# Constants on GpSimd, an early loop entry on VectorE, and V's last half in smaller pieces, in a one-query attention over 8192 keys

## The chip, the cores and the metric

The kernel runs on one core of a Trainium2 chip. The metric is the device time of one execution in microseconds (us). The profile is of one execution, and its span is 1.8 us shorter than the time of that execution.

Five engines do the work: TensorE (PE; its weight loads are PEld), VectorE (DVE), ScalarE (ACT), GpSimd (POOL), and SyncE (SP), which here only issues DMAs. Sixteen DMA engines move the data (the page counts in shares of 16, and a piece has 16 landing records).

## The reference

```python
B, H, Sq, Sk, D = 1, 16, 1, 8192, 256          # all bfloat16

def reference(q, k, v):
    scale = q.shape[-1] ** -0.5
    scores = jnp.einsum("bhqd,bhkd->bhqk", q, k) * scale
    p = _softmax(scores, axis=-1)
    return jnp.einsum("bhqk,bhkd->bhqd", p, v)
```

There is one query per head, so every byte of K and V is used once: 16 heads x 2 tensors x 8192 x 256 x 2 bytes = 134.2 MB must be read. There is nearly no arithmetic per byte.

## The kernel before

Each head's K and V are read in two halves of 2 MB. A half lies in SBUF as 128 partitions x 32 columns x 256 elements. The 64 halves go through one issue queue (SyncE): four K halves first, then K and V in turn. There are four K buffers and four V buffers. Some halves are cut into pieces (the numbers are columns):

```python
FIRST_CUT = (4, 4, 8, 16)     # the first half of K
LAST_CUT = (16, 8, 4, 4)      # the last half of V
BEFORE_CUT = (16, 16)         # two V halves before it
...
for i, wd in enumerate(cs):   # one DMA per piece, all from SyncE
    plan.op("sp", lambda e, ...: e.dma_start(
        b[:, at * D : (at + wd) * D], cols(t, h, c + at, c + at + wd)), ..., waits, dma=(s, used[id(s)]))
```

VectorE takes 24 of 32 columns of each K half (product with the broadcast query and a sum, one instruction a column), TensorE the other eight (transposes and matmuls). Then come the softmax over the head's 8192 scores and 64 matmuls with V. VectorE's part is a loop of eight passes over two heads. Ahead of it, VectorE makes the constants that the other engines need (ones, and two identity matrices for TensorE):

```python
dve(lambda e: e.memset(ones_rowb[:, :], 1.0), "c_onesb")
...                                              # an index row by doubling, a transpose, a compare
dve(lambda e: e.tensor_scalar(identb[:, :], colf[:, :], pidx[:, 0:1], None, ALU.is_equal), "c_idb", ["c_p"])
dve(lambda e: e.tensor_scalar(ident[:, :], colf[:, :], pidx[:, 0:1], None, ALU.is_equal), "c_id")
...
with nc.Fori(0, n, 1, engines=[eng.engine], head_slot={eng.engine: 0}):
    for j in range(step):
        ...                                      # the loop's waits and instructions
```

`head_slot` sets the place of the loop's first instruction in the engine's stream of instructions; the code ahead of the loop branches there (VectorE's at 4.43 us in the trace below).

The matmuls with a V half wait piece by piece; `landed` names the pieces that a column needs:

```python
for c in range(c0, c1):
    pe(lambda e, c=c, col=col: e.matmul(a[0:1, 0:D], lhsT=E[:, col : col + 1],
           rhs=Vb[slot][:, c * D : (c + 1) * D], ...),
       ..., [f"e{h}", first_free] + landed("v", n, c, c + 1))
```

## Time and profile before

| what | value | where |
|---|---|---|
| time | 324.89 us, median of 3 | the runs |
| VectorE busy | 277.7 us, 86% | page, part 1 |
| TensorE busy | 220.3 us, 68% | page, part 1 |
| DMA queue of K and V | 98.2% of 16 engines' span | page, part 3 |
| VectorE's first product | 10.75 us | timeline |

From the page of the kernel before: the share of busy DMA engines and the bytes per second in 40 slices of the span, then the K and V queue (packets, MB, share of 16 engines), then the chain of work that ended last.

```profile
DMA  7999999999999999999999999999999999999993
GB/s 276 431 432 424 419 435 430 424 422 430 426 429 430 424 424 430 430 430 428 424 430 428 432 428 422 430 428 429 430 424 426 428 429 435 424 422 432 417 419 128
...
q1 hardware_dynamic: 10368, 134.22, 98.2%
...
DVE 49%; DMA 42%; issue 5%; PE 3%; DVEq 0%; ACT 0%; SPq 0%
```

Two lines here contradict each other. By the queue, the DMA engines are full from the second slice to the last but one. By the chain, half of the span is VectorE's. Both are right as records. The chain goes back from a DMA to what released its issue (VectorE freeing a K buffer), although that DMA then waited in a full queue, which the chain doesn't see (K half 4, issued at 19.36 us, before K half 3 landed, at 22.34 to 24.53). The packet records of this kernel give 428.5 GB/s between 285 and 300 us, if each packet's bytes are spread over its time (the profile's table of stretches, which counts a packet whole where it starts, says 433).

VectorE's start, from the timeline (start, duration, engine, line, operation, and in brackets the idle time before it and what ended it):

```profile
0.81 0.17 DVE L279 MEMSET ones_rowb<- 1x128 bf16 x1 [0.81 <-PEq L728]
...
3.82 0.06 DVE L298 MEMSET lsum<- 128x1 f32 x1
10.75 0.42 DVE L360 CUSTOM_DVE_ANT_0 prod<-Kb,qbc 128x256 bf16<-128x256 bf16 x1 [6.88 <-issue]
```

"issue" means that it waited for nothing that the profile shows. In the records of its sequencer there is a taken branch at 4.43 us and nothing until 10.6.

The DMA issues of the beginning, from the timeline of SyncE. The first row merges eight issues; its last is K half 4, the first that needs a freed buffer, at 19.36 us:

```profile
0.73 18.95 SPq L319 DMA_DIRECT2D Kb<-in_k_dram  x8
19.73 0.43 SPq L319 DMA_DIRECT2D Vb<-in_v_dram  x1
```

The tail, from the timeline of TensorE:

```profile
312.50 3.95 PE L607 MATMUL acc<-Vb,E 128*1 128x256 bf16 x32
317.05 3.65 PE L607 MATMUL acc<-Vb,E 128*1 128x256 bf16 x32 [0.59 <-DMA Vb<-in_v_dram]
```

The last piece landed at 319.50 us, and TensorE ended at 320.70, 1.20 us later. It was held until 317.05 by a piece of 16 columns and then had 32 matmuls to do, 0.109 us each.

### The profile page before, as it was taken

The numbers are of one execution on the slowest core, as the hardware profiler recorded it, in microseconds if no ns is written. First come the engines' busy times: TensorE is split into PE (matmuls) and PEld (weight loads), VectorE is DVE, ScalarE is ACT, GpSimd is POOL, SyncE is SP. The second block draws the span as 40 slices with busy tenths as digits, with TensorE's granted clock in tenths as the row PEclk, the third lists the DMA queues.
The fourth block names the chain that finished last, engine by engine and source line by source line (L and its number), as shares of the span: only waits on it lengthen the run. The fifth ranks groups of instructions, "written<-read, shape, count | busy, mean of one in ns | idle before, by whom it ended". The sixth has DMA issues, their size and how long they took to land.

```text
span 322.8 us, 6456 instructions
## 1 busy us (share of the span) xinstructions
PE 220.3 (68%) x2166; PEld 155.1 (48%) x2166; DVE 277.7 (86%) x1607; ACT 94.1 (29%) x185; POOL 0.2 (0%) x4
## 2 busy tenths in 40 slices
PE   1463428777587848784887658686667866857896
PEld 0332325545456635563565535464444644535574
DVE  3699999999999999999998988889988889888600
ACT  3362321423324242332142242212422213232010
POOL 0000000000000000000000000000000000000000
PEclk9999999979789967999597987977898796998799
DMA  7999999999999999999999999999999999999993
GB/s 276 431 432 424 419 435 430 424 422 430 426 429 430 424 424 430 430 430 428 424 430 428 432 428 422 430 428 429 430 424 426 428 429 435 424 422 432 417 419 128
DMA packets 10415, 134.37 MB, mean 416 GB/s; under 512 B 1170, under 2 KB 1187, under 8 KB 1956
## 3 DMA queue, kind: packets, MB, share of 16 engines
q1 hardware_dynamic: 10368, 134.22, 98.2%
q8 instruction: 5, 0.08, 0.1%
q14 instruction: 6, 0.05, 0.0%
q10 hardware_dynamic: 36, 0.02, 0.0%
HBM read 134.23 MB, written 0.01 MB: 416 GB/s over the span
## 4 chain that ended last, share of the span: by engine, by line
DVE 49%; DMA 42%; issue 5%; PE 3%; DVEq 0%; ACT 0%; SPq 0%
DVE prod L360 46%; DMA Kb<-in_k_dram 27%; DMA Vb<-in_v_dram 15%; PE acc L607 3%; DVE S L360 2%; DVE g L332 0%; DVE colf L286 0%; DVE recip L341 0%; DVE m L379 0%; DVEq L145 0%; ACT o L621 0%; DVEq L138 0%; SPq L319 0%; DVEq L139 0%; DVEq L142 0%
## 5 line engine op out<-in xcount | busy, mean ns | idle before, releaser
L360 DVE CUSTOM_DVE_ANT_0 prod<-Kb,qbc 128x256 bf16<-128x256 bf16 x768 | 269.1, 411 | 24.5 <-DMA Kb<-in_k_dram 15.1
L607 PE MATMUL acc<-Vb,E 128*1 128x256 bf16 x1024 | 144.7, 310 | 8.7 <-DMA Vb<-in_v_dram 8.5
L607 PEld LDWEIGHTS acc<-Vb,E 128*1 128x1 bf16 x1024 | 95.0, 95 | 50.7 <-DMA Vb<-in_v_dram 9.9
L502 ACT ACTIVATE KT<-tp 128x1024 bf16<-128x1024 bf16 x64 | 62.0, 1021 | 118.3 <-PE tp L493 118.3
L360 DVE DVE_READ_ACCUMULATOR2_ANT S<- 128x1 f32 x768 | 56.5, 74 | 0.0
L493 PE MATMUL tp<-identb,Kb 128*128 128x128 bf16 x512 | 38.9, 237 | 7.1 <-DMA Kb<-in_k_dram 7.1
L493 PEld LDWEIGHTS tp<-identb,Kb 128*128 128x128 bf16 x512 | 33.0, 106 | 15.2 <-issue 12.8
L519 PE MATMUL spe<-qcur,KT 128*128 128x1 bf16 x512 | 20.7, 165 | 19.6 <-ACT KT L502 19.6
L558 PE MATMUL misc<-g,ones_row 1*128 1x1 f32 x32 | 7.3, 294 | 35.0 <-DVE g L332 35.0
L519 PEld LDWEIGHTS spe<-qcur,KT 128*128 128x128 bf16 x512 | 16.5, 99 | 24.5 <-ACT KT L502 24.3
L621 ACT ACTIVATE o<-acc,recip 1x256 bf16<-1x256 f32 x16 | 7.4, 465 | 68.7 <-PE acc L607 68.7
L558 PEld LDWEIGHTS misc<-g,ones_row 1*128 1x128 f32 x32 | 5.9, 229 | 38.1 <-DVE g L332 37.8
L547 PE MATMUL misc<-ident,m 128*1 128x128 f32 x34 | 7.1, 293 | 20.4 <-DVE m L379 20.4
L547 PEld LDWEIGHTS misc<-ident,m 128*1 128x1 f32 x34 | 1.9, 82 | 24.0 <-DVE m L379 23.5
L565 ACT ACTIVATE negb<-misc 128x1 f32<-128x1 f32 x16 | 2.7, 171 | 26.0 <-PE misc L558 26.0
L332 DVE TENSOR_REDUCE g<-misc 1x1 f32<-1x128 f32 x17 | 4.7, 274 | 5.2 <-PE misc L547 5.2
L587 PE MATMUL misc<-ones_col,lsum 128*1 128x1 f32 x34 | 3.2, 164 | 5.5 <-ACT E L572 3.6
L572 ACT ACTIVATE E<-S,negb 128x64 bf16<-128x64 f32 x16 | 5.6, 347 | 0.7 <-ACT negb L565 0.2
L341 DVE RECIPROCAL recip<-misc 1x1 f32<-1x1 f32 x17 | 2.6, 151 | 3.7 <-PE misc L587 3.7
L439 ACT ACTIVATE qbc<-qb 128x256 bf16<-128x256 bf16 x14 | 5.6, 399 | 0.0
L532 ACT ACTIVATE S<-spe 128x16 f32<-128x16 f32 x16 | 3.0, 184 | 7.2 <-PE spe L519 7.2
L422 ACT ACTIVATE qb<-tp 128x512 bf16<-128x512 f32 x7 | 3.9, 595 | 3.8 <-PE tp L413 3.8
(29 smaller groups left out, 23.0 us busy)
## 6 DMA issues: line engine op xcount, KB each, us to landing
Kb<-in_k_dram SPq DMA_DIRECT2D x31, 2048.0 KB, 23.7
Vb<-in_v_dram SPq DMA_DIRECT2D x29, 2048.0 KB, 29.2
Vb<-in_v_dram SPq DMA_DIRECT2D x5, 1024.0 KB, 19.0
Kb<-in_k_dram SPq DMA_DIRECT2D x1, 1024.0 KB, 7.1
Kb<-in_k_dram SPq DMA_DIRECT2D x2, 256.0 KB, 2.9
Kb<-in_k_dram SPq DMA_DIRECT2D x1, 512.0 KB, 4.7
Vb<-in_v_dram SPq DMA_DIRECT2D x1, 512.0 KB, 12.8
Vb<-in_v_dram SPq DMA_DIRECT2D x2, 256.0 KB, 13.1
```

The source lines that it names most:

```text
L332: lambda e: e.tensor_reduce(g[0:1, s : s + 1], misc[s][0:1, MT0 : MT0 + P], AX.X, ALU.max),
L360: lambda e, slot=slot, c=c, col=col, h=h, r=(ttr - 1) % PROD: e.tensor_tensor_reduce(out=prod[:, r * D : (r + 1) * D], in0=Kb[slot][:, c * ...
L422: lambda e: e.activation(out=qbc[:, a * D : b * D] if first else qb[:, (a - 2) * D : (b - 2) * D], in_=bank[:, 0 : (b - a) * D], func=ACT. ...
L439: lambda e: e.activation(out=qbc[:, s * D : (s + 1) * D], in_=qb[:, (h - 2) * D : (h - 1) * D], func=ACT.Copy),
L493: lambda e, c=c, hf=hf, i=(b * NH + hf) * P, view=view: e.transpose(view[:, i : i + P], Kb[slot][:, c * D + hf * P : c * D + (hf + 1) * P] ...
L502: lambda e, gn=gn, view=view: e.activation(out=KT[gn % KT_SLOTS][:, :], in_=view[:, 0 : GROUP * D], func=ACT.Copy),
L519: lambda e, b=b, hf=hf, oc=oc, gn=gn: e.matmul(spe[sl(h)][:, oc : oc + 1], lhsT=KT[gn % KT_SLOTS][:, (b * NH + hf) * P : (b * NH + hf + 1) ...
L547: lambda e: e.matmul(misc[s][0:1, MT0 : MT0 + P], lhsT=m[:, s : s + 1], rhs=ident[:, :], start=True, stop=True),
L558: lambda e: e.matmul(misc[s][:, BC0 : BC0 + 1], lhsT=ones_row[0:1, :], rhs=g[0:1, s : s + 1], start=True, stop=True),
L572: lambda e: e.activation(out=E[:, s * J : (s + 1) * J], in_=S[:, s * J : (s + 1) * J], func=ACT.Exp, bias=negb[:, h : h + 1], scale=SCALE, ...
L607: lambda e, c=c, col=col: e.matmul(a[0:1, 0:D], lhsT=E[:, col : col + 1], rhs=Vb[slot][:, c * D : (c + 1) * D], start=(x == 0 and c == 0), ...
L621: lambda e: e.activation(out=o[0:1, h * D : (h + 1) * D], in_=acc[s][0:1, 0:D], func=ACT.Copy, scale=recip[0:1, s : s + 1],),
```

## The change

The change wants VectorE free of preparatory work and of the gap before its loop, and the last data in pieces that let TensorE keep up. GpSimd, idle so far, makes the constants, with one `iota` (column minus partition) and two compares with zero. VectorE's loop head goes to slot 128. V's last half is cut so that no piece is over eight columns. The rest is bookkeeping: GpSimd gets an instruction stream, and VectorE's counter starts at 32 so that the loop's register waits stay positive.

```diff
-LAST_CUT = (16, 8, 4, 4)
+LAST_CUT = (8, 8, 8, 4, 4)
+HEAD_SLOT = {"pe": 0, "dve": 128}
 ...
+        if e in self.ahead:
+            eng.sem_inc(self.sems[e], self.ahead[e])
 ...
-            with nc.Fori(0, n, 1, engines=[eng.engine], head_slot={eng.engine: 0}):
+            with nc.Fori(0, n, 1, engines=[eng.engine], head_slot={eng.engine: HEAD_SLOT[e]}):
 ...
-        dve(lambda e: e.memset(ones_rowb[:, :], 1.0), "c_onesb")
-        ...                                   (all constants of VectorE)
-        dve(lambda e: e.memset(lsum[:, 1:2], 1.0), "e-1")
+        pool(lambda e: e.memset(ones_rowb[:, :], 1.0), "c_onesb")
+        pool(lambda e: e.iota(off[:, :], pattern=[[1, P]], base=0, channel_multiplier=-1, ...), "c_off")
+        pool(lambda e: e.tensor_scalar(identb[:, :], off[:, :], 0.0, None, ALU.is_equal), "c_idb", ["c_off"])
+        pool(lambda e: e.tensor_scalar(ident[:, :], off[:, :], 0.0, None, ALU.is_equal))
+        ...                                   (four memsets)
 ...
+        plan.ahead["dve"] = 32
+            @block.gpsimd
+            def _(e):
+                plan.emit("pool", e)
```

## The prediction

> **What bounds the kernel now.** The DMA engines. The page's queue table gives q1 98.2% of 16 engines' span; the slices show 419 to 435 GB/s from the second slice to the last but one. In the packet records a 16 KB packet takes 611 ns, and from 5 to 312 us 15 or more are practically always in flight: the engines never idle. Each 2 MB piece lands 4.89 us after the last. So the time is: first packet (about 2 us after the start), 134.2 MB at that pace, and a tail. The chain of waits says otherwise (DVE 49%), because it walks through freed K buffers; but K half 4, issued at 19.36 us, still found K half 3 in flight (landing 22.3 to 24.5).
>
> **VectorE enters at once.** The timeline shows VectorE's constants from 0.81 to 3.82 us, register moves until 4.4, a taken branch at 4.43, and nothing until 10.6:[...] (an 8,192-byte instruction packet at 8.79 us, under load).[...] VectorE should start when q's broadcast is ready, at about 3.9 us instead of 10.75: 6.9 us earlier. None of this is on the DMA engines' path: K half 4 is issued near 12.5 instead of 19.4 us, into a queue that is full anyway. Worth: 0.
>
> **A side effect that may count.** The 16 engines do not end together: a piece's 16 landings spread over 1.5 us at K half 1, 2.2 at K half 2, 3.0 at V half 0, and 3.2 at the end. Its steps coincide with instruction packets at 8.79, 13.90 and 33.23 us[...]. The slowest engine gains about 0.9 us of lag at each of the three. One fetch fewer should leave that engine near 2.2 us of lag, so that the next, at 2.6, ends last: estimate 0.5 us off the last landing.
>
> **The last half in pieces.** In the timeline the last 16-column piece lands at 317.00, and TensorE then runs 32 matmuls back to back (0.109 us apart) to 320.70, although the later pieces landed at 318.21, 318.86 and 319.50. With 8 columns first, landing about 315.8, TensorE keeps up and has about 4 matmuls left after the last landing: 0.45 us saved. Eight more packets per engine: estimate 0.07 us.
>
> **GpSimd's constants.** Its memsets take 0.1 us[...]. TensorE needs the identity by about 9.2 us (K transposes start 9.28, when the data lands). Slack enough.
>
> **Sum.** 0.5 + 0.45 - 0.07 = 0.9 us, of 324.89: 324.0 us, range 323.2 to 324.9. Faster by over 2%: 0.01; within 2%: 0.98; slower: 0.01.
>
> **To look for.** VectorE's first product near 3.9 us; 4.89 us per piece unchanged; no instruction packet near 8.8; spread of the last landings about 2.6 us instead of 3.2; TensorE's end about 0.7 us after the last landing instead of 1.2.
>
> **What would make it wrong.** No fetch saved (then 324.4), or it moved to an engine that is late already; a slow iota that stalls both TensorE and VectorE beyond 20 us, when the DMA queue would run dry.

0.5 + 0.45 - 0.07 = 0.88, given as 0.9 us. The 0.07 us for eight packets agrees with the trace before: two packets of 2,048 bytes took 9 ns longer than one of 4,096 (84 and 159 ns, medians), and eight times that is 72 ns. "Fetch" means an 8,192-byte packet that the trace calls an instruction packet. No record names which of the five engines it serves; that these are VectorE's is the author's reading of their times (8.79 us, within VectorE's gap of 4.43 to 10.6).

## The result, and the profile after

The changed kernel took 324.27 us (median of 6 runs, 323.32 to 325.07), the kernel before 325.12 us (median of 6, 324.76 to 326.18). The ratio is 0.9969, with a 95% interval of 0.9948 to 0.999. A ratio in this document is the mean time of one kernel's fast runs over that of the other's in the same rounds, so it is not quite the ratio of the medians that are quoted beside it. The difference itself, about 0.85 us, is small but clear of noise.

The profiled execution happened to be the slowest of the six (325.07 us), so its span of 323.3 us is longer than that of the profile before (322.8). A single trace against a single trace would say that the change does harm.

From the page of the changed kernel, the same lines:

```profile
DMA  7999999999999999999999999999999999999993
GB/s 230 431 438 423 424 430 432 426 424 424 431 432 428 424 432 428 432 426 426 434 430 428 424 428 432 430 430 421 428 432 430 430 423 434 426 428 430 416 417 142
...
q1 hardware_dynamic: 10512, 134.22, 98.2%
...
DMA 56%; DVE 38%; PE 2%; issue 2%; SPq 1%; DVEq 0%; ACT 0%
```

The stream is what it was. Only the first slice differs: 230 GB/s instead of 276. In the chain VectorE's share fell by 11 points and the DMA's rose by 14, but the time has not moved with it.

VectorE's start, the constants on GpSimd, and SyncE's first issues, from the timelines:

```profile
4.09 0.42 DVE L359 CUSTOM_DVE_ANT_0 prod<-Kb,qbc 128x256 bf16<-128x256 bf16 x1 [4.09 <-ACT qbc L421]
```

```profile
0.95 0.23 POOL L286 IOTA off<- 128x128 f32 x1
1.27 0.54 POOL L291 TENSOR_SCALAR identb<-off 128x128 bf16<-128x128 f32 x1
1.77 0.53 POOL L292 TENSOR_SCALAR ident<-off 128x128 f32<-128x128 f32 x1
```

```profile
0.72 13.50 SPq L318 DMA_DIRECT2D Kb<-in_k_dram  x8
14.26 0.43 SPq L318 DMA_DIRECT2D Vb<-in_v_dram  x1
```

VectorE starts 6.7 us earlier, and K half 4 is issued at 13.89 us instead of 19.36. What became of the 6.7 us is in VectorE's waits (total us, times, longest). Before, then after:

```profile
DVE prod L360 <- DMA Kb<-in_k_dram: 15.1, 13, 1.2
DVE prod L360 <- issue: 9.4, 5, 6.9
```

```profile
DVE prod L359 <- DMA Kb<-in_k_dram: 22.9, 20, 1.6
DVE prod L359 <- issue: 1.9, 3, 0.7
```

Its waits without a visible cause, the loop's entry above all, fell by 7.5 us; its waits for K grew by 7.8 us. VectorE, early for data that come at a fixed pace (here 4.89 us a half), only waits somewhere else. In these two traces its last product even ends later after the change (304.31 us) than before (303.31).

The tail of the changed kernel, from TensorE's weight loads, which show its two short waits:

```profile
315.53 3.36 PEld L604 LDWEIGHTS acc<-Vb,E 128*1 128x1 bf16 x32 [0.41 <-DMA Vb<-in_v_dram]
319.29 1.61 PEld L604 LDWEIGHTS acc<-Vb,E 128*1 128x1 bf16 x16 [0.40 <-DMA Vb<-in_v_dram]
```

Here the last piece landed at 320.53 us and TensorE ended at 321.20, 0.67 us later instead of 1.20.

### The profile page after: what moved, and what is told of

Same layout as the page of the kernel before. It is cut to its first block, busy times and chain, and to the rows that moved or that the text cites. A ratio compares the mean times of both kernels' runs of the same rounds, so it can differ in the third digit from the quotient of the medians.

```text
span 323.3 us, 6446 instructions
## 1 busy us (share of the span) xinstructions
PE 223.0 (69%) x2166; PEld 155.7 (48%) x2166; DVE 275.6 (85%) x1586; ACT 94.1 (29%) x185; POOL 1.9 (1%) x12
## 3 DMA queue, kind: packets, MB, share of 16 engines
q1 hardware_dynamic: 10512, 134.22, 98.2%
## 4 chain that ended last, share of the span: by engine, by line
DMA 56%; DVE 38%; PE 2%; issue 2%; SPq 1%; DVEq 0%; ACT 0%
DMA Kb<-in_k_dram 41%; DVE prod L359 36%; DMA Vb<-in_v_dram 15%; PE acc L604 2%; DVE S L359 1%; SPq L318 1%; DVE g L331 0%; DVE recip L340 0%; ACT o L618 0%; DVE m L378 0%; DVEq L150 0%; DVEq L147 0%; DVEq L144 0%
## 5 line engine op out<-in xcount | busy, mean ns | idle before, releaser
L604 PE MATMUL acc<-Vb,E 128*1 128x256 bf16 x1024 | 148.2, 315 | 9.4 <-DMA Vb<-in_v_dram 9.0
L604 PEld LDWEIGHTS acc<-Vb,E 128*1 128x1 bf16 x1024 | 96.5, 96 | 53.5 <-DMA Vb<-in_v_dram 10.7
L490 PE MATMUL tp<-identb,Kb 128*128 128x128 bf16 x512 | 38.2, 234 | 9.0 <-DMA Kb<-in_k_dram 8.9
L490 PEld LDWEIGHTS tp<-identb,Kb 128*128 128x128 bf16 x512 | 32.3, 105 | 17.1 <-issue 14.4
L412 PE MATMUL tp<-q,identb 16*128 16x256 bf16 x15 | 4.2, 406 | 1.0 <-ACT qb L421 0.5
## 6 DMA issues: line engine op xcount, KB each, us to landing
Vb<-in_v_dram SPq DMA_DIRECT2D x3, 512.0 KB, 11.6
```

The source lines that it names most:

```text
L412: lambda e, i=i, src=src: e.matmul(bank[:, i * D : (i + 1) * D], lhsT=src[0], rhs=src[1], start=True, stop=True),
L490: lambda e, c=c, hf=hf, i=(b * NH + hf) * P, view=view: e.transpose(view[:, i : i + P], Kb[slot][:, c * D + hf * P : c * D + (hf + 1) * P] ...
```

## The experiments

My theory: the DMA engines bound everything, so only three things count: how soon the 16 engines are full, how far the last of them lags, and what TensorE still has to do after the last landing. Rival A: VectorE is on the critical path, as the chain shows. Rival B, formed after the first trace with its thinner start: something in the change disturbs the first DMAs, and gives back part of the gain.

One table serves all runs. "Rate" is the DMA rate from 5 to 7 us, in GB/s, as the profile's table of stretches has it. "Half 0" is the mean landing time of the 16 engines' shares of the last piece of K's first half. "Fetches" counts the 8,192-byte instruction packets in the first 40 us. "Spread" is the time from the first to the last of the 16 landings of the last piece. "Tail" is TensorE's end minus the last landing. All times are in us; "time" and "before" are medians of the same job.

| run | iota on GpSimd | first product | rate | half 0 | fetches | spread | tail | time | before | ratio (95%) |
|---|---|---|---|---|---|---|---|---|---|---|
| before | no | 10.75 | 365 | 8.32 | 3 | 3.05 | 1.20 | | | |
| the change | yes | 4.09 | 264 | 9.21 | 2 | 3.36 | 0.67 | 324.27 | 325.12 | 0.9969 (0.9948-0.999) |
| r1_after_again | yes | 4.23 | 326 | 8.87 | 2 | 2.28 | 0.69 | 324.28 | 325.00 | 0.9981 (0.9966-0.9997) |
| r1_cut_only | no | 10.06 | 377 | 8.54 | 3 | 4.06 | 1.19 | 324.63 | 325.00 | 0.9987 (0.9972-1.0002) |
| r1_entry_only | yes | 4.17 | 238 | 9.05 | 2 | 3.11 | 1.22 | 324.62 | 325.00 | 0.9989 (0.9972-1.0006) |
| r1_slot0 | yes | 6.13 | 295 | 9.02 | 3 | 2.54 | 0.67 | 324.26 | 325.00 | 0.9986 (0.997-1.0003) |
| r2_old_consts_slot128 | no | 5.15 | 348 | 8.51 | 2 | 2.51 | 1.18 | 324.45 | 325.04 | 0.9975 (0.9956-0.9993) |
| r2_late_slot128 | yes | 11.61 | 291 | 8.87 | 2 | 2.75 | 0.68 | 324.28 | 325.04 | 0.9971 (0.9954-0.9988) |
| r2_late_slot0 | yes | 17.24 | 326 | 8.78 | 3 | 1.66 | 0.69 | 327.82 | 325.04 | 1.0067 (1.0046-1.0089) |
| r2_first16 | yes | 5.93 | 422 | 7.95 | 2 | 2.11 | 1.12 | 323.06 | 325.04 | 0.993 (0.9914-0.9946) |
| r3_before_first16 | no | 9.88 | 434 | 7.79 | 3 | 2.86 | 1.18 | 324.25 | 325.16 | 0.9972 (0.9958-0.9985) |
| r3_first32 | yes | 8.87 | 463 | 7.92 | 2 | 1.96 | 0.69 | 323.04 | 325.16 | 0.9935 (0.9921-0.9949) |
| r3_idle_iota | yes | 5.17 | 262 | 9.07 | 2 | 3.28 | 1.20 | 325.29 | 325.16 | 1.0003 (0.9986-1.002) |
| r3_idle_memsets | no | 5.29 | 358 | 8.46 | 2 | 3.03 | 1.23 | 324.83 | 325.16 | 0.9996 (0.998-1.0013) |

(The table of stretches counts a packet's bytes and time whole in the stretch in which the packet starts, so in a short stretch a rate or a DMA share can come out a little too high, the share over 1.)

The runs named r1, r2 and r3 are three jobs on three chips; "before" was run again in each, but the changed kernel only in the first job and in r1. Differences of a few tenths of a microsecond between jobs are not read.

### The changed kernel once more

No edit.

> The changed kernel once more, to see which differences between the two first traces repeat. If the DMA engines bound the time, it is again about 0.9 us faster than before (ratio 0.997). The first trace of the changed kernel had a dip of the DMA rate between 4.5 and 8 us (212 to 330 GB/s, where before had 310 to 420) that put every later landing back by 0.85 us. If VectorE's early start makes this dip, this trace has it too, with K half 1 landing at 13.3 us or later on the fastest engine (before: 12.57). If it is chance, this trace may lack it, and then the span is about 0.8 us shorter than 323.3.

The gain repeats: 324.28 against 325.00 us. So does the thinner start, in part: half 0 at 8.87 us (first trace 9.21, before 8.32). The spread at the end does not repeat: 2.28 instead of 3.36 us. The spread is a matter of the single execution, of up to a microsecond, and it makes most of the difference between these two traces (last landing 319.71 against 320.53).

### The last half's pieces alone

```diff
 (the kernel before)
-LAST_CUT = (16, 8, 4, 4)
+LAST_CUT = (8, 8, 8, 4, 4)
```

> The kernel before with V's last half in pieces of 8, 8, 8, 4 and 4 columns, nothing else. Theory (DMA engines bound the time, the tail is TensorE catching up): TensorE ends 0.7 us after the last landing instead of 1.2, so 0.45 us faster, ratio 0.9986. Rival (the chain of waits through VectorE is the bound): the same gain, as the tail is the same; the rival differs in the next run.

By its median it gained 0.37 us, with an interval that just holds zero. Its trace does not show the shorter tail (1.19 us), though the tail is 0.67 to 0.69 in five other kernels with these pieces. The timeline of TensorE in this run tells why:

```profile
314.62 0.19 PE L587 MATMUL misc<-ones_col,lsum 128*1 128x1 f32 x2
314.68 7.15 PE L607 MATMUL acc<-Vb,E 128*1 128x256 bf16 x64
```

The last 64 matmuls run in one go, without a wait: TensorE was behind the data. It had waited 1.89 us for V half 27 (to 300.81 us), and then some 27 matmuls came 0.213 us apart instead of 0.109. In the two traces of the changed kernel the wait was 1.58 and 1.32 us, and some 16 matmuls were slow. The slow ones stand where the profile has TensorE's granted clock at half: for 6.8 us here (299.6 to 306.4), for 3.4 us in each trace of the changed kernel (300.9 to 304.3). From the table of stretches (stretch, length, busy time of PE, PEld, DVE, ACT and POOL with counts, granted clock, DMA share, GB/s), first this run, then the changed kernel:

```profile
297.00:309.00 12.00, 8.89 (x67) 5.83 (x68) 7.67 (x46) 2.17 (x4) 0.00 (x0) 0.72 1.00 421
```

```profile
297.00:309.00 12.00, 9.19 (x81) 6.36 (x79) 7.54 (x45) 2.35 (x4) 0.00 (x0) 0.86 0.99 417
```

The finer pieces pay only while TensorE keeps up with the data; in the changed kernel's trace it has some 0.8 us to spare (the two waits of 0.41 and 0.40 us above). The run with K's first half in two pieces (below) also has 6.8 us at half clock at this place (297.4 to 304.3 us), as many slow matmuls and a long tail. Both profiled executions were the slowest runs of their kernels (325.78 us, the next 324.81; 323.55, the next 323.11). This points to the execution and not to the edit as the cause of the long tail, but neither kernel was profiled twice, and what decides when the clock is halved was not looked into.

### Constants and entry alone

```diff
 (the changed kernel)
-LAST_CUT = (8, 8, 8, 4, 4)
+LAST_CUT = (16, 8, 4, 4)
```

> The changed kernel with V's last half in the old pieces of 16, 8, 4 and 4 columns: constants on GpSimd and VectorE's early start alone. Theory: VectorE starts near 4 us instead of 10.75 and gains between 0 and 0.5 us (the 0.5 only if a saved instruction fetch was on the engine that lands last). Rival A (VectorE is on the critical path, as the chain of waits shows it with 49%): 2 to 6 us faster, ratio 0.98 to 0.994. Rival B (early VectorE work disturbs the first DMA pieces): slower than before by up to 0.8 us, ratio up to 1.0025.

It gained 0.38 us by the median, not clear of zero, although VectorE started 6.6 us earlier. Rival A is out: 2 to 6 us were its claim, and the interval ends at 0.9 us. The two parts, 0.37 and 0.38, sum to 0.75, and the whole change measured 0.72 in the same job; as neither part is clear of zero, the agreement says little.

### The loop head at slot 0 again

```diff
 (the changed kernel)
-HEAD_SLOT = {"pe": 0, "dve": 128}
+HEAD_SLOT = {"pe": 0, "dve": 0}
```

> The changed kernel with VectorE's loop head at slot 0 again: constants on GpSimd and the new pieces stay, [...]VectorE should stall at the branch for some us and start at 6 to 10 us. Theory: three instruction fetches of 8,192 bytes in VectorE's first 35 us instead of two, time within 0.5 us of the changed kernel. Rival A: slower by the late start, 2 to 6 us. Rival B (early VectorE work disturbs the DMA): no dip at 4.5 to 8 us, and faster than the changed kernel by up to 0.8 us.

VectorE's sequencer branched at 1.86 us and went on at 5.99: the entry stall is back, with 4.1 us. The time is that of the changed kernel (324.26 against 324.28). In this company the new slot was worth nothing that six runs can tell. The dip at 5 us is still there although VectorE's first product comes only at 6.13, so VectorE's products cannot make it. That left GpSimd's constants and the early fetch.

### VectorE's constants, with the loop head at slot 128

```diff
 (the kernel before)
-head_slot={eng.engine: 0}
+head_slot={eng.engine: 128 if e == "dve" else 0}
```

> The kernel before with VectorE's loop head at slot 128 and nothing else: VectorE makes the constants itself, GpSimd stays idle, and the loop is entered without a fetch, at about 4.6 us instead of 10.75. In the four traces in which VectorE is early and GpSimd makes the constants the last K-half-0 piece lands on average at 8.87 to 9.21 us, in the two others at 8.32 and 8.54. If VectorE's early work or its early instruction fetch costs the first DMA pieces, this trace has 9.0 as well. If GpSimd's constants cost it, this trace has 8.4. Time: the theory that DMA bounds everything says within 0.5 us of before, ratio 0.998 to 1.002.

With VectorE early but GpSimd idle there is no dip: 348 GB/s, half 0 at 8.51 us. The loop was entered without a stall (first product 5.15 us). It gained 0.59 us, clear of zero; constants and entry together gained 0.38 in another job, not clear of it. The run r3_idle_memsets below is the same kernel but for seven memsets on GpSimd that nobody reads, and gained 0.33 us by the median (ratio 0.9996, 0.998 to 1.0013), so the 0.59 is not confirmed. GpSimd is not needed for the early start, since VectorE's own constants are done at 3.87 us and the broadcast query comes at about 4.

### VectorE held back

```diff
 (the changed kernel; for r2_late_slot0 also "dve": 0 in HEAD_SLOT)
+        dve(lambda e: e.nop(), None, ["k0.3"])     # before the loop: wait until K's first half is there
```

> The changed kernel with VectorE held before its loop until K half 0 has landed (a no-op that waits), so that it starts near 9.4 us; GpSimd still makes the constants, the head is still at slot 128. If VectorE's early work costs the first DMA pieces, their last lands on average near 8.4 us; if GpSimd's constants or something else of the change do, near 9.0. Time: within 0.6 us of the changed kernel; a rival that has VectorE on the critical path expects it 5 us slower.

VectorE started at 11.61 us, later than in the kernel before, and the time was 324.28 us, within the noise that of the changed kernel (also 324.28 in its job). The early start, for which the change was made, is worth nothing that can be measured here. The dip is there without VectorE's early work, so it is not VectorE's; nor is it the early fetch's, for the first 8,192-byte instruction packet of this run comes at 14.77 us.

> As the run before, but with the head at slot 0, so that no instruction fetch of VectorE falls before 9 us and VectorE starts as late as in the kernel before or later (10 to 14 us). If the early fetch at 4 to 5 us costs the first DMA pieces, this run has 8.4 us and the run before has 9.0; if GpSimd's constants do, both have 9.0; if VectorE's early products do, both have 8.4. Time: within 0.7 us of the changed kernel.

Here I expected too little. The held VectorE also met the stall at the loop's entry (branch at 11.29 us, next record 17.10), and started at 17.24. K half 4 was then issued at 25.85 us, when the last of the engines had finished K half 3 at 24.89. From the table of stretches:

```profile
24.00:25.00 1.00, 0.87 (x9) 0.60 (x6) 1.00 (x7) 0.94 (x2) 0.00 (x0) 1.00 0.00 0
25.00:27.00 2.00, 1.32 (x20) 1.01 (x20) 2.00 (x13) 1.27 (x5) 0.00 (x0) 1.00 0.39 82
```

No packet was in flight for 2.3 us, and the run took 3.5 us longer than the changed kernel. This is where the critical path begins: VectorE's start may be late, at no cost, as long as K half 4 is issued before the queue is empty. At 10.75 us (issue at 19.36) the kernel before was still on the safe side.

This run shows one thing more. When the queue ran dry, all engines began again together, so their later lags can be read one by one, against the instruction packets. From the landing records (piece, first and last of the 16 landings, spread) and the packet records:

```
K half 4   32.56..33.05  spread 0.48
V half 0   37.45..37.94  spread 0.48
           instruction packet 16,384 B at 38.0 us, 8,192 B at 39.8 us
K half 5   42.34..44.13  spread 1.80   (the next engine 1.26, the others 0.82 or less)
           instruction packet 16,384 B at 46.6 us
V half 1   47.29..49.20  spread 1.92   (a second engine 1.74)
```

The records don't name the DMA engine of a packet. But where the instruction packets stand, single engines step back against the others by some 0.7 to 1.4 us, and don't catch up: the spread is still 1.98 us at 106 us. The page counts instruction packets and data in the time of the same 16 engines (q1 with the data 97.4%, q8 with the 16,384-byte instruction packets 0.1%); how an engine divides its time between them is not shown.

### Whose is the thin start?

```diff
 (the kernel before, head at slot 128; GpSimd's results are read by nothing)
+        plan.op("pool", lambda e: e.memset(scr2[:, 0:1], 1.0))                          # r3_idle_iota
+        plan.op("pool", lambda e: e.iota(scr[:, :], pattern=[[1, P]], base=0, channel_multiplier=-1, ...))
+        for i in range(6):                                                              # r3_idle_memsets
+            plan.op("pool", lambda e: e.memset(scr[:, :], 1.0), f"p{i}", [f"p{i - 1}"] if i else [])
+        plan.op("pool", lambda e: e.memset(scr2[:, :], 1.0))
```

> Whose is the thinner start of the DMA? In the runs with GpSimd's constants K half 0 lands on average at 8.78 to 9.21 us and 2.56 to 2.74 MB are moved by 10 us; without them at 8.32 to 8.54 us and 2.83 to 2.93 MB. This is the kernel before with VectorE's loop head at slot 128 and VectorE's own constants, and GpSimd makes one iota[...] into a tile that nothing reads. If the iota[...] do it: 8.8 us or later and under 2.75 MB. If not: 8.3 to 8.6 us.

> The same, but GpSimd makes seven memsets of 128x128 instead[...] for 1 to 2 us, into tiles that nothing reads. If any GpSimd work at the start thins the DMA: 8.8 us or later and under 2.75 MB by 10 us. If it takes the iota[...]: 8.3 to 8.6 us and over 2.8 MB here, and 8.8 in the run before.

The stretch from 5 to 7 us in the table of stretches, for before, the changed kernel, the iota alone and the memsets alone:

```profile
5.00:7.00 2.00, 0.00 (x0) 0.00 (x0) 0.00 (x0) 0.00 (x0) 0.00 (x0) 1.00 0.96 365
```

```profile
5.00:7.00 2.00, 0.02 (x1) 0.00 (x0) 1.95 (x12) 0.00 (x0) 0.00 (x0) 1.00 0.89 264
```

```profile
5.00:7.00 2.00, 0.00 (x0) 0.00 (x0) 1.83 (x11) 0.00 (x0) 0.00 (x0) 1.00 0.91 262
```

```profile
5.00:7.00 2.00, 0.10 (x1) 0.00 (x0) 1.71 (x9) 0.10 (x1) 0.00 (x0) 1.00 0.96 358
```

One iota of 0.24 us, whose result nobody reads, thins the DMA 4 us later as much as the whole change does; seven memsets (1.7 us) don't. Over all the traces with the old first pieces the two groups are apart: with an iota half 0 lands at 8.78 to 9.21 us (seven traces), without at 8.32 to 8.54 (four). The delay of some half a microsecond stays: K half 20 lands on average at 185.6 to 185.9 us in those of these traces with an iota and at 185.2 to 185.3 without (r2_late_slot0, where the queue ran dry, left out). In time, this job gives 325.29 us with the iota and 324.83 with the memsets, but with four runs each the ranges overlap (324.82 to 325.79, 324.77 to 325.57), so the cost in time is not shown.

In the changed kernel's trace two instructions named MODIFY_POOL_CONFIG stand just ahead of the iota, at 0.87 and 0.90 us; the run with memsets alone has none. What they do is not shown: no instruction queue of the DMA table grows from the kernel before to the changed one (q8 five packets in both, q14 six and then five), and they and the iota were not tried apart. So it is shown that an iota on GpSimd, with what comes ahead of it, thins the start of the DMA (262 GB/s instead of 358 from 5 to 7 us, half 0 at 9.07 us instead of 8.46), and not how.

### Larger first pieces

```diff
 (the changed kernel for r2_first16 and r3_first32, the kernel before for r3_before_first16)
-FIRST_CUT = (4, 4, 8, 16)
+FIRST_CUT = (16, 16)          # r3_first32: (32,)
```

> The changed kernel with K's first half in two pieces of 16 columns instead of 4, 4, 8 and 16. If the DMA engines bound the time, VectorE's later start (it must wait for 1 MB, near 5 us) costs nothing, and larger packets with fewer issues fill the engines earlier: by 10 us about 0.3 MB more are moved than the 2.6 MB of the changed kernel, and the time falls by 0.3 to 1.0 us, ratio to before 0.994 to 0.997. If VectorE's start matters, it is slower than the changed kernel by about 1 us.

> The kernel before with K's first half in two pieces of 16 columns, nothing else. VectorE's start is not moved: it still stalls at the loop's entry until about 10 us. If the DMA engines bound the time, it is still 0.8 to 1.5 us faster than before (ratio 0.9955 to 0.9975), from the earlier filling of the engines alone. If the gain of the run with these pieces needs VectorE's early start, nothing is gained here (0.999 to 1.001).

> The changed kernel with K's first half in one piece of 2 MB. VectorE cannot start before it lands, near 8 us, so it gives up 4 us of the change's early start. If the DMA engines bound the time and K half 4 is still issued (near 17 us) before the queue runs dry (near 22 us), it is within 0.4 us of the version with pieces of 16 (323.06): ratio to before 0.992 to 0.995. If VectorE's start counts, it is 2 us or more slower than that.

If VectorE's start doesn't count, small first pieces have no purpose; and they may cost, because their packets are short (2,048 bytes in 84 ns, against 16,384 bytes in 613 ns, both medians of the trace before) and a DMA is issued only about every 0.47 us. The two reasons were not tried apart. From the page and the table of stretches of the changed kernel with two pieces of 16:

```profile
GB/s 300 441 428 419 426 428 432 430 428 426 425 428 428 428 430 432 428 426 428 428 430 432 430 426 428 426 428 432 427 432 426 430 423 430 430 428 432 416 414 153
```

```profile
5.00:7.00 2.00, 0.71 (x3) 0.09 (x2) 1.07 (x7) 0.55 (x3) 0.00 (x0) 1.00 1.02 422
```

The first slice has 300 GB/s instead of 230, and half 0 lands at 7.95 us instead of 9.21. VectorE starts 1.8 us later than in the changed kernel, and the kernel is 1.2 us faster: 323.06 us, against 324.28 for the changed kernel in its job and for r2_late_slot128 in this one. With one piece of 2 MB VectorE gives up nearly 5 us of its early start (8.87 us), and the time is the same, 323.04. On the kernel before the larger pieces alone give 0.91 us, as much as the whole change, with VectorE's late start untouched. The dip is gone too: with large pieces the iota costs little (7.95 and 7.92 with it, 7.79 without).

Both versions with larger pieces beat the kernel before and the changed one. In the run with two pieces TensorE was behind at the end, as in the run with the new last pieces alone, and again at half clock before it:

```profile
312.53 7.15 PE L604 MATMUL acc<-Vb,E 128*1 128x256 bf16 x64
```

So TensorE's tail is the next thing that would bind, in executions like this one.

## Why the prediction was right

The time was right: 324.0 forecast, 324.27 measured, within 323.2 to 324.9. The gain forecast was 0.9 us; it measured 0.85 in the first job and 0.72 in the second. The steps do not all stand.

- **The DMA engines bound the time, and the chain misleads.** Right. The rate is the same before and after the change once the queue is full (428.5 GB/s from 285 to 300 us by the packet records of both), and VectorE's first product at 4.2, 6.1 or 11.6 us (the changed kernel, slot 0, held back) gives 324.28, 324.26 and 324.28 us.
- **VectorE enters at once; worth 0.** Right. Its start was forecast near 3.9 us and measured 4.09. K half 4 was issued at 13.89 instead of the forecast 12.5, since VectorE waited for the thinner first pieces. The stall goes with the slot: at slot 128 the sequencer goes on 0.57 us after the branch with the constants on VectorE (r2_old_consts_slot128), and at slot 0 after 4.1 to 6.2 us, in five traces with either maker of constants. An 8,192-byte instruction packet falls within each of the five stalls and none between the branch and the loop in that run at slot 128, but that VectorE waits for this packet is not shown.
- **One fetch fewer cuts the spread to about 2.6 us, worth 0.5.** Not confirmed. One fetch is indeed saved, two instead of three, and an engine does step back where a fetch stands (in the trace before, the spread is 1.50 us at K half 1 and 2.19 at K half 2, with one at 13.90 us). But the 16 KB instruction packets do the same (above, a second engine from 1.26 to 1.74 us with one at 46.6 us; no record says which of the five engines they serve), and how these lags add up differs from run to run: the spread of the last piece was 2.54 to 4.06 us in the four traces with three fetches where the queue stayed full, and 1.96 to 3.36 in the nine with two. In time the saved fetch shows in one comparison (slot 128 alone, 0.59 us) and not in the others (the same with idle memsets, 0.33 and not clear of zero; slot 128 against slot 0 with GpSimd's constants, 0.0).
- **The finer last pieces, 0.38 net.** Right in size by the medians: 0.37 alone, and 0.34 on top of constants and entry, neither clear of zero. The tail is 0.67 us, forecast 0.7. What I had not seen is that TensorE may be late by itself, when its granted clock is halved just before the end.
- **GpSimd's constants: slack enough.** The iota and the compares took 1.35 us, from 0.95 to 2.30. Right that nobody waits, though the reason was off: TensorE first uses the identity at 3.26 us and not near 9.2 (in the kernel before at 3.91); it was ready at 1.81, so the slack was 1.4 us. The step also took it that what no engine waits for costs nothing. The iota thins the first DMAs (262 GB/s instead of 358), which puts the later landings back by about 0.5 us on average.

So that the forecast sum was right is partly luck: it counted a gain at the end that is not reliably there, and it left out a delay at the start that was not foreseen. That these two offset each other is argued from the traces and not shown in time. The worth of the saved fetch alone stays open at this noise; some tenths of a microsecond would need many more runs.

## What to carry to other kernels

When the DMA queue never runs empty (here 98.2% of 16 engines' span), ask of each change only whether it fills the engines sooner, keeps them full, or shortens what follows the last landing; here VectorE, freed earlier, waited elsewhere (7.8 us more for K), although the chain of waits gave it half of the span. And here an early start of VectorE was worth less than large first pieces: cutting the first 2 MB less finely gave at least as much as the whole change (0.91 us against 0.85). And in effects below 1% repeat the profile before reading it: the spans of two traces of one kernel differed by 0.8 us, as much as the change brought.
